# Strassen kernel for a gated FNet and FFN mix: second-level couples moved from product 3 to product 4 of the output stage, evictions at high priority, a longer warm-up of short matmuls

## The chip, the cores and the metric

The kernel runs on one core of a Trainium2 chip. The metric is the device time of one execution in microseconds (us), lower is better; a run's time includes about 2 us outside the span that the profile covers. All times here are of the chip.

## What is computed

The reference mixes two transforms of the same x (2048 x 1024) row by row with a gate; F is 3584:

```python
x = A_x                                                  # S = 2048, D = 1024
g = _sigmoid((x * gate_w).sum(-1, keepdims=True))
# A: real part of a DFT over the hidden dimension, then over the sequence
a = jnp.einsum("bsd,ed->bse", x, dft_hid_re)
b = jnp.einsum("bsd,ed->bse", x, dft_hid_im)
y = jnp.einsum("ts,bse->bte", dft_seq_re, a) - jnp.einsum("ts,bse->bte", dft_seq_im, b)
# B: dense, squared relu, dense
h = jnp.einsum("bsd,df->bsf", x, w1) + b1
h = jnp.where(h > 0, h, 0) ** 2
out = jnp.einsum("bsf,fd->bsd", h, w2) + b2
return g * y + (1 - g) * out
```

All of it is in fp32.

## The kernel before

**Precision.** Each operand is split into a high part (`hi`, rounded to the matmul format by ScalarE, L220) and the rest (`lo`, by VectorE, L230). A product of two operands is three matmuls, hi·hi, hi·lo and lo·hi (L299 to L304), each of a 128x128 stationary and a 128x512 moving tile into a PSUM tile `ps`. Narrow operands of 256 columns hold both parts in one tile, `both`: its first half is written by ScalarE, its second by VectorE.

**Strassen.** Every stage multiplies with the seven products of Strassen and Winograd, in the order 1, 2, 5, 6, 3, 7, 4 (L19). Operands of a product are blocks or sums of blocks (S1 to S4, T1 to T4), made by VectorE (L172) from loaded blocks (L152, SyncE's queue). Results of a product are added to output blocks that stay in SBUF. Some products use a second level of Strassen on some couples of the inner dimension K (`twice`): `TWICE_O = {2: 3, 3: 3}` (L20) says that in the output stage products 2 and 3 do so on 3 couples each. The stage has 7 steps of K, hence 3 couples and one step left over. A couple at the second level saves 12 of 96 matmuls. The rest of a product goes step by step (`direct`), a step being 24 matmuls.

**Stages.** In order: the DFT over the hidden dimension (1224 matmuls), the DFT over the sequence ("spectral stage", `c_stage`, 2580, with the second level on 4 couples in product 2, 3 in product 3 and 2 in product 4), the first dense layer in two parts (1224 and 936), the second dense layer ("output stage", `o_stage`, 2280). Together 8244 matmuls of L304. Ahead of them stand 8 matmuls on a tile of ones (`WARM`, L905), which compute nothing that is used.

**Second level of a product, in two phases** (`twice`). First phase: k couples, each as four steps of 12 matmuls, into four groups (second-level products 1, 6, 7, 5). As each group ends, its PSUM block goes to the output: product 1 by ScalarE's copy to a temporary u (L490) and VectorE's add (L444), product 6 and 7 each by two adds (L501, then L503), product 5 by L444, L526 and L529. Second phase: three groups (products 2, 3, 4) and the steps that are left, on PSUM tiles that are first filled ("prefilled") from those output blocks by ScalarE (L292), so that TensorE adds on top of them. For this place the text speaks of the switch of a product.

**Evictions.** When a group ends, its callback (`done`) is run from `Group.run`: ScalarE copies PSUM to SBUF (`put`, L438 and, in the wide stages, L606), VectorE adds PSUM to a block (`add`, L444 and L613), or the block is finished: `final` (L841 twice, L844, then a store from GpSimd's queue, L943), and in the last group of the output stage `last` row by row (L828, L830 and a store each, L831). `Group.prepare` takes PSUM tiles and prefills them.

**Order.** The main loop (L916 to L973) goes through the steps; at each it issues loads, sums and splits of later steps as planned costs and free slots allow (`SLOTS` 55 tiles), then the step's matmuls. The tile framework's scheduler then orders each engine's instructions by priority, which follows the order of the program unless a block asks for another. Engines run their instructions in order; a waiting instruction holds all behind it on its engine.

**Far sums.** With `FAR_TALL = ("T2",)`, sum T2 of a right operand is stored to DRAM by GpSimd's queue when it is made and loaded again when a later sum needs it (L127, `far`); `early("T4")` (L466 to L467) instead makes T4 during product 6 and stores that, for the first 2·k steps of K if product 4 has k couples at the second level.

Of the kernel before, what the change touches and what calls it, by code (L numbers as in the profile page):

```python
# [11 lines left out]
AF = mybir.ActivationFunctionType  # L12
ALU = mybir.AluOpType

P = 128
# [1 line left out]
NF = F // P  # L17
SLOTS, KEEP, RAWS = 55, 5, 4
WIDE, TALL_C, TALL_O = ((1, 2, 5, 6, 3, 7, 4),) * 3  # L19
TWICE_X, TWICE_C, TWICE_O = (1, 2, 5, 3, 4), {2: 4, 3: 3, 4: 2}, {2: 3, 3: 3}  # L20
LATER = 3
WARM = 8
FAR_TALL, FAR_WIDE = ("T2",), ()
TWICE_H = (1, 2, 5, 3, 4), (2, 5, 3, 4)
SUMS, RESTS, LOADS, SPREAD = 3, 2, 12, 9
# [16 lines left out]
def gated_mix_kernel(ctx: ExitStack, tc: tile.TileContext, x4, xn, w4, ct, w1a, w1b, w2, b1, b2, gw, out):  # L42
# [11 lines left out]
    nc = tc.nc  # L54

    const = ctx.enter_context(tc.tile_pool(name="const", bufs=1))
# [49 lines left out]
    class View:  # L106
# [6 lines left out]
        done = property(lambda self: self.base.done)  # L113
# [150 lines left out]
    class Group:  # L264


        def __init__(self, rows, k, *done, onto=None, sign=1, by_row=False):

            self.sign, self.per = float(sign), 1 if by_row else 2
# [6 lines left out]
        def prepare(self):  # L279

            if not all(b.begun for b in self.onto or ()):
                return
            for k in range(len(self.ps), -(-self.rows // self.per)):
                if not banks or self.per == 2 and len(banks) < -(-self.rows // 2) - k:
                    break
                self.pools.append(banks.popleft())
                t = self.pools[-1].tile([P, 2, 512], F32, name="ps", tag="ps")
                self.ps.append(t)
                if self.onto:
                    n = min(self.per, self.rows - self.per * k)  # L290
                    at = self.per * k % 2
                    nc.scalar.activation(t[:, :n, :], self.onto[self.per * k // 2].slot[:, at:at + n, :], AF.Copy,  # L292
                                         scale=self.sign)

        def run(self, st, mv, by_part=False):
            self.prepare()
            self.at += 1
            ends = self.at % self.k == 0
            mms = [(r, kk, n) for r in range(self.rows) for kk in range(2) for n in range(3)]  # L299
            if by_part:  # L300
                mms.sort(key=lambda e: (e[1], e[0] // 2, e[2], e[0]) if e[1] == 0 else (e[1], e[2], e[0]))
            for r, kk, n in mms:
                a, b = ((st.hi, mv.hi), (st.hi, mv.lo), (st.lo, mv.hi))[n]
                nc.tensor.matmul(self.ps[r // self.per][:, r % self.per, :], a[:, kk, r * P:(r + 1) * P],  # L304
                                 b[:, kk, :], start=self.at == 1 and kk + n == 0 and not self.onto,
                                 stop=ends and kk == 1 and n == 2,
                                 skip_group_check=bool(self.at > self.k or self.onto))
                if ends and self.per == 1 and kk == 1 and n == 2:
                    self.done[0][0](r // 2, self.ps[r], r % 2)
                elif ends and (r % 2 or r == self.rows - 1) and kk == 1 and n == 2:  # L310
                    self.done[self.at // self.k - 1][0](r // 2, self.ps[r // 2])
            if self.at == self.k * len(self.done):
                banks.extend(self.pools)

# [49 lines left out]
    def seven(order, second, new_u, c11, c12, c21, c22, put, add, direct, twice, slots, sign=1):  # L364

        one, u = new_u(), new_u()
        before = {p: order[:order.index(p)] for p in order}

        def product(p, old, new, ends, slots, drop=False, sign=1):
            if p in second:  # L370
                twice(p, old, new, ends, drop, sign)
                return

            def take_up(k, ps):
                put(new, k, ps, ends, sign)
                if drop:
                    old[k].drop()

            direct(p, old, slots, take_up, [new], sign)

        def six(k, ps):
            put(u, k, ps)
            add(c12, k, ps, 3 in before[6], c22, sign)
            if 2 in before[6]:
                one[k].drop()

        def seven(k, ps):
            add(c22, k, ps, True, None, sign)
            if 4 in before[7]:
                add(c21, k, ps, True)  # L390
                u[k].drop()
            else:
                put(u, k, ps)

        ends = {}
        for p in order:
            if p == 1:
                product(1, None, one, False, slots)
            elif p == 2:
                product(2, one, c11, True, slots, 6 in before[2])  # L400
            elif p == 3:
                product(3, c12, c12, True, 0, sign=sign)
            elif p == 4 and 7 in before[4]:
# [12 lines left out]
        return ends  # L416

    def tall(left, right, ksteps, order, second, target, final, last=None):
# [10 lines left out]
        c11, c12, c21, c22 = ({k: target(i, n, k) for k in keys} for i in range(2) for n in range(2))  # L429
# [18 lines left out]
                near.done = True  # L448
                later.append((now[0] + LATER, lambda: final(near, None)))

        def direct(p, onto, slots, take_up, into, sign):
            l, r = FACTORS[p]
            end = last and p == order[-1]

            def take_row(rp, ps, row):
                last(into[0][1, rp], ps, row)
                if row:
                    onto[1, rp].drop()

            groups = [Group(4, ksteps, (take_row if end and c else lambda rp, ps, c=c: take_up((c, rp), ps), slots,  # L460
                                        [d[c, rp] for d in into for rp in range(2)]),
                            onto=onto and [onto[c, rp] for rp in range(2)], by_row=end and c) for c in range(2)]
# [115 lines left out]
    def wide(left, right, rows, order, second, target, final, sign=1, onto_old=False):  # L578
# [14 lines left out]
        c11, c12, c21, c22 = ({k: target(i, n, k) for k in keys} for i in range(2) for n in range(2))  # L593
# [24 lines left out]
                near.done = True  # L618
                later.append((now[0] + LATER, lambda: final(near, None, 1)))

        def direct(p, onto, slots, take_up, into, sign):
            l, r = FACTORS[p]
            mvs = [[right[q, c].operand(r) for q in range(2)] for c in range(2)]
            for m in range(2):
                sts = [left[m, q].operand(l, rows * P) for q in range(2)]
                for c in (m, 1 - m):
                    group = Group(rows, 2, (lambda rp, ps, m=m, c=c: take_up((m, c, rp), ps), slots,
                                             [d[m, c, rp] for d in into for rp in range(2)]),
                                  onto=onto and [onto[m, c, rp] for rp in range(2)], sign=sign)
                    for q in range(2):  # L630
                        step(sts[q], mvs[c][q], group)

# [228 lines left out]
    at, rows = c_stage()  # L861
# [13 lines left out]
    n = len(steps)  # L875
# [26 lines left out]
    nc.vector.memset(ones, 1.0)  # L902
    idle = banks[-1].tile([P, 2, 512], F32, name="ps", tag="ps")
    for _ in range(WARM):
        nc.tensor.matmul(idle[:, 0, :], ones[:, :P], ones, start=True, stop=True)  # L905
# [105 lines left out]
```

## Time and profile before

| | before |
|---|---|
| median of 3 runs | 1890.89 us (1890.39 to 1891.28) |
| profiled execution, its time | 1891.5 us |
| its span | 1889.6 us |
| TensorE busy | 1878.5 us, 99% |
| VectorE busy | 1610.7 us, 85% |
| ScalarE busy | 999.9 us, 53% |
| mean DMA rate over the span | 234 GB/s |

In the profile PE is TensorE's matmuls, PEld its weight loads, DVE VectorE, ACT ScalarE, POOL GpSimd, SP SyncE; a name with q is an engine's queue of DMA issues. A row of the timeline has the start and length in us, the engine, line and operation, the tiles written and read, the shape and the count of instructions merged; in brackets the idle time before it and what released it. A matmul's length reaches over the start of the next one, so rates are read from starts. A row of a wait lists the total, the times and the longest. Stages by first matmul: the first stage at 6.1 us, the spectral stage at 288, the dense layer's parts at 876 and 1153, the output stage at 1367 with its products 2 at 1443, 5 at 1511, 6 at 1588, 3 at 1664, 7 at 1732 and 4 at 1808 to 1884.

### The profile page before, as it was taken

To read this page: it belongs to the slowest core of one execution; us is meant where nothing else is said; L and a number is where in the kernel's file an instruction comes from. 1 tells how busy PE (TensorE), PEld (TensorE's weight loads), DVE (VectorE), ACT (ScalarE), POOL (GpSimd) and SP (SyncE) were. 2 spreads that over 40 slices of the span, in tenths; PEclk is the share of its full clock that TensorE was granted. 3 is DMA by queue.
4 is the path that set the end of the run, shared out by engine and by line. 5 is a ranking of instruction groups with operands and counts; after the bars stand their busy time and mean duration, and the time that the engine had idled before them with its cause. 6 is when DMAs were issued, how large, how long until landed. Compare 5 with 4: busy or idle time off the path is not lost.

```text
span 1889.6 us, 21909 instructions
## 1 busy us (share of the span) xinstructions
PE 1878.5 (99%) x8252; PEld 1548.7 (82%) x8252; DVE 1610.7 (85%) x1543; ACT 999.9 (53%) x1123; POOL 86.8 (5%) x161
## 2 busy tenths in 40 slices
PE   9999999999999999999999999999999999999998
PEld 6888888888888878888888888888888888888887
DVE  8998899499778998798896997989976996699883
ACT  7474564363243554455484797667954434364440
POOL 0000110000000000000000000000100000000000
PEclk9999999999999999999999999999999999999999
DMA  5732889339687489483452865627863886549971
GB/s 223 259 110 88 345 294 407 132 114 378 257 307 263 154 306 357 172 312 112 164 189 71 330 215 199 225 89 294 292 260 100 316 334 241 188 157 361 410 307 45
DMA packets 128425, 442.93 MB, mean 234 GB/s; under 512 B 14128, under 2 KB 23616, under 8 KB 128320
## 3 DMA queue, kind: packets, MB, share of 16 engines
q1 hardware_dynamic: 106272, 363.13, 53.0%
q0 software_dynamic: 21472, 77.61, 10.4%
q8 instruction: 65, 1.06, 0.2%
q10 hardware_dynamic: 576, 0.79, 0.1%
q14 instruction: 40, 0.33, 0.1%
HBM read 362.83 MB, written 78.65 MB: 234 GB/s over the span
## 4 chain that ended last, share of the span: by engine, by line
PE 54%; issue 40%; POOL 2%; ACT 1%; DVE 1%; DMA 1%; SPq 0%; POOLq 0%; DVEq 0%; ACTq 0%
PE ps L304 54%; POOL h L127 1%; ACT hi L220 1%; DVE lo L230 1%; DMA raw<-in_x 0%; DMA raw<-in_ct 0%; POOL copy L127 0%; POOL gy L127 0%; DMA h<-h 0%; DVE h L613 0%; ACT u L606 0%; DVE o L828 0%; DVE o L830 0%; DVE raw L172 0%; SPq L152 0%
## 5 line engine op out<-in xcount | busy, mean ns | idle before, releaser
L304 PE MATMUL ps<-hi 128*128 128x512 f32 x2328 | 906.1, 390 | 2.6 <-ACT u L606 1.1
L304 PE MATMUL ps<-lo,hi 128*128 128x512 f32 x2328 | 905.4, 389 | 0.0
L304 PE MATMUL ps<-hi,lo 128*128 128x512 f32 x2328 | 904.6, 389 | 0.7 <-DVE lo L230 0.6
L220 ACT ACTIVATE hi<-raw 128x1024 fp32r<-128x1024 f32 (+2 forms) x413 | 419.9, 1037 | 410.2 <-DVE raw L172 268.0
L230 DVE TENSOR_TENSOR lo<-raw,hi 128x1024 fp32r<-128x1024 f32 (+2 forms) x413 | 484.6, 1200 | 57.1 <-ACT hi L220 33.0
L304 PEld LDWEIGHTS ps<-hi 128*128 128x128 f32 x2328 | 437.3, 188 | 95.9 <-ACT hi L220 2.7
L304 PEld LDWEIGHTS ps<-hi,lo 128*128 128x128 f32 x2328 | 437.4, 188 | 93.1 <-DVE lo L230 2.2
L304 PEld LDWEIGHTS ps<-lo,hi 128*128 128x128 f32 x2328 | 437.5, 188 | 90.7 <-DVE lo L230 0.2
L172 DVE TENSOR_TENSOR raw<-raw 128x1024 f32<-128x1024 f32 (+1 forms) x276 | 326.6, 1207 | 55.8 <-DMA raw<-in_ct 19.7
L220 ACT ACTIVATE hi<-sum 128x1024 fp32r<-128x1024 f32 (+1 forms) x172 | 175.5, 1035 | 194.6 <-DVE sum L172 151.4
L304 PE MATMUL ps<-hi,both 128*128 128x512 f32 x840 | 260.5, 390 | 1.2 <-ACT ps L292 1.2
L230 DVE TENSOR_TENSOR lo<-sum,hi 128x1024 fp32r<-128x1024 f32 (+1 forms) x172 | 203.4, 1199 | 32.4 <-ACT hi L220 24.9
L304 PEld LDWEIGHTS ps<-hi,both 128*128 128x128 f32 x840 | 157.7, 188 | 35.9 <-ACT ps L292 2.6
L304 PE MATMUL ps<-lo,both 128*128 128x512 f32 x420 | 163.7, 390 | 0.1
L172 DVE TENSOR_TENSOR sum<-raw 128x1024 f32<-128x1024 f32 (+1 forms) x116 | 122.2, 1067 | 36.9 <-PE ps L304 31.6
L172 DVE TENSOR_TENSOR sum<-raw,sum 128x1024 f32<-128x1024 f32 (+2 forms) x87 | 96.8, 1120 | 14.4 <-PE ps L304 11.6
L606 ACT ACTIVATE u<-ps 128x1024 f32<-128x1024 f32 x76 | 72.0, 952 | 69.2 <-PE ps L304 60.9
L613 DVE TENSOR_TENSOR h<-h,ps 128x1024 f32<-128x1024 f32 x92 | 98.1, 1086 | 11.8 <-ACT u L606 10.0
L304 PEld LDWEIGHTS ps<-lo,both 128*128 128x128 f32 x420 | 78.8, 188 | 16.7 <-DVE lo L230 0.5
L292 ACT ACTIVATE ps<-u 128x1024 f32<-128x1024 f32 (+1 forms) x74 | 70.2, 954 | 27.2 <-DVE o L841 10.5
L710 ACT ACTIVATE h<-h,b1c 128x512 f32<-128x512 f32 x112 | 74.3, 712 | 6.1 <-DVE h L613 5.8
L220 ACT ACTIVATE both<-sum 128x512 fp32r<-128x512 f32 x60 | 37.1, 623 | 45.5 <-DVE sum L172 32.1
(61 smaller groups left out, 648.1 us busy)
## 6 DMA issues: line engine op xcount, KB each, us to landing
raw<-in_ct SPq DMA_DIRECT2D x151, 512.0 KB, 6.5
raw<-h SPq DMA_DIRECT2D x132, 512.0 KB, 7.1
raw<-in_x SPq DMA_DIRECT2D x107, 512.0 KB, 5.3
raw<-in_w SPq DMA_DIRECT2D x98, 512.0 KB, 6.4
raw<-ab SPq DMA_DIRECT2D x72, 512.0 KB, 6.6
h<-h POOLq DMA_DIRECT2D x48, 512.0 KB, 5.4
raw<-in_w1a SPq DMA_DIRECT2D x36, 512.0 KB, 5.4
ab<-ab POOLq DMA_DIRECT2D x32, 512.0 KB, 6.5
```

Source lines behind the costliest of these rows:

```text
L127: nc.gpsimd.dma_start(self.at[:, k:k + tiles, :], src[:, :tiles, :])
L172: nc.vector.tensor_tensor(self.slot[:, k, c], src[0][:, k, c], src[1][:, k, c], op=self.op)
L220: nc.scalar.activation(self.hi[:, k, c], self.block.slot[:, k, c], AF.Copy)
L230: nc.vector.tensor_tensor(self.lo[:, k, c], self.block.slot[:, k, c], self.hi[:, k, c].bitcast(F32), op=SUB)
L292: nc.scalar.activation(t[:, :n, :], self.onto[self.per * k // 2].slot[:, at:at + n, :], AF.Copy, scale=self.sign)
L304: nc.tensor.matmul(self.ps[r // self.per][:, r % self.per, :], a[:, kk, r * P:(r + 1) * P], b[:, kk, :], start=self.at == 1 and kk + n == ...
L606: nc.scalar.activation(view(near.slot, k), view(ps, k), AF.Copy, scale=float(sign))
L613: nc.vector.tensor_tensor(view(near.slot, k), view((src or dst)[k].slot, k), view(ps, k), op=ADD if sign > 0 else SUB)
L710: nc.scalar.activation(dst.slot[:, k, :], (dst.slot if ps is None else ps)[:, k, :], AF.Relu, bias=b1c[:, tile0 + k:tile0 + k + 1])
```

## The change

Five things are changed together.

1. `TWICE_O` becomes `{2: 3, 3: 2, 4: 2}`: in the output stage product 3 has the second level on 2 couples of K, not 3, and product 4, the last one, on 2, not on none. The last group of the kernel, finished row by row, is then the second level's block (1, 1) with 2 rows; before it was a half of product 4 with 4 rows. T4 is made early, in product 6, for 4 steps of K.
2. `WARM` becomes 44, on a tile of ones of 128x128: each warming matmul has 128 columns, not 512.
3. Evictions (the callbacks `done`) and ScalarE's prefills are issued under `tc.high_priority(100)`.
4. A block that a group is prefilled from is dropped when it has been copied to PSUM (`spend`), not when the group's result is taken up; the slots that product 7 asks for change accordingly.
5. The first loads go out in another order and on other queues: w part 0, x part 1, w part 1 and x part 2 on SyncE's, x part 0 on ScalarE's; before, both w parts and x part 2 on SyncE's, x parts 0 and 1 on ScalarE's.

```diff
-TWICE_X, TWICE_C, TWICE_O = (1, 2, 5, 3, 4), {2: 4, 3: 3, 4: 2}, {2: 3, 3: 3}
+TWICE_X, TWICE_C, TWICE_O = (1, 2, 5, 3, 4), {2: 4, 3: 3, 4: 2}, {2: 3, 3: 2, 4: 2}
 LATER = 3
-WARM = 8
+WARM = 44
+AHEAD, AHEAD_P = 100, 100
...
-        def __init__(self, rows, k, *done, onto=None, sign=1, by_row=False):
+        def __init__(self, rows, k, *done, onto=None, spend=False, sign=1, by_row=False):
...
-                    nc.scalar.activation(t[:, :n, :], self.onto[self.per * k // 2].slot[:, at:at + n, :], AF.Copy,
-                                         scale=self.sign)
+                    b = self.onto[self.per * k // 2]
+                    with tc.high_priority(AHEAD_P):
+                        nc.scalar.activation(t[:, :n, :], b.slot[:, at:at + n, :], AF.Copy, scale=self.sign)
+                    if self.spend and (self.per == 2 or at):
+                        b.drop()
...
-                if ends and self.per == 1 and kk == 1 and n == 2:
-                    self.done[0][0](r // 2, self.ps[r], r % 2)
-                elif ends and (r % 2 or r == self.rows - 1) and kk == 1 and n == 2:
-                    self.done[self.at // self.k - 1][0](r // 2, self.ps[r // 2])
+                if not (ends and kk == 1 and n == 2):
+                    continue
+                with tc.high_priority(AHEAD):
+                    if self.per == 1:
+                        self.done[0][0](r // 2, self.ps[r], r % 2)
+                    elif r % 2 or r == self.rows - 1:
+                        self.done[self.at // self.k - 1][0](r // 2, self.ps[r // 2])
...
-                direct(6, one, 2 * slots, six, [u, c12], 1)
+                direct(6, one, 2 * slots, six, [u, c12], 1, 2 in before[6])
             else:
-                direct(7, u, 0, seven, [u, c22, c21], 1)
+                direct(7, u, slots * (4 not in before[7]), seven, [u, c22, c21], 1, True)
...
-    run(first[0].load_parts(cycle((nc.sync,))), first[2].load_parts(iter((nc.scalar, nc.scalar, nc.sync))))
-    ones = const.tile([P, 512], mybir.dt.bfloat16, name="ones")
+    w_parts, x_parts = first[0].load_parts(cycle((nc.sync,))), first[2].load_parts(iter((nc.scalar, nc.sync, nc.sync)))
+    for parts in (w_parts, x_parts, x_parts, w_parts, x_parts):
+        next(parts)
+    run(w_parts, x_parts)
+    ones = const.tile([P, P], mybir.dt.bfloat16, name="ones")
     nc.vector.memset(ones, 1.0)
     idle = banks[-1].tile([P, 2, 512], F32, name="ps", tag="ps")
     for _ in range(WARM):
-        nc.tensor.matmul(idle[:, 0, :], ones[:, :P], ones, start=True, stop=True)
+        nc.tensor.matmul(idle[:, 0, :P], ones, ones, start=True, stop=True)
```

More of the change, by code (lines that the diff above doesn't have):

```diff
@@ L264, in gated_mix_kernel @@
     class Group:
-        def __init__(self, rows, k, *done, onto=None, sign=1, by_row=False):
-            self.sign, self.per = float(sign), 1 if by_row else 2
+        def __init__(self, rows, k, *done, onto=None, spend=False, sign=1, by_row=False):
+            self.sign, self.per, self.spend = float(sign), 1 if by_row else 2, spend
             self.rows, self.k, self.done, self.at, self.onto = rows, k, done, 0, onto
@@ L372, in product @@
                 return
[L374 to L379, printed above, removed]
+            direct(p, old, slots, lambda k, ps: put(new, k, ps, ends, sign), [new], sign, drop)
         def six(k, ps):
@@ L383, in six @@
             add(c12, k, ps, 3 in before[6], c22, sign)
-            if 2 in before[6]:
-                one[k].drop()
         def seven(k, ps):
@@ L390, in seven @@
                 add(c21, k, ps, True)
-                u[k].drop()
             else:
@@ L449, in add, with direct @@
                 later.append((now[0] + LATER, lambda: final(near, None)))
-        def direct(p, onto, slots, take_up, into, sign):
+        def direct(p, onto, slots, take_up, into, sign, spend=False):
             l, r = FACTORS[p]
             end = last and p == order[-1]
[L455 to L460, printed above, removed]
+            groups = [Group(4, ksteps, ((lambda rp, ps, row: last(into[0][1, rp], ps, row)) if end and c else
+                                        lambda rp, ps, c=c: take_up((c, rp), ps), slots,
                                         [d[c, rp] for d in into for rp in range(2)]),
-                            onto=onto and [onto[c, rp] for rp in range(2)], by_row=end and c) for c in range(2)]
+                            onto=onto and [onto[c, rp] for rp in range(2)], spend=spend, by_row=end and c) for c in range(2)]
             sts = {q: left[q].operand(l) for q in range(ksteps)}
@@ L619, in add, with direct @@
                 later.append((now[0] + LATER, lambda: final(near, None, 1)))
-        def direct(p, onto, slots, take_up, into, sign):
+        def direct(p, onto, slots, take_up, into, sign, spend=False):
             l, r = FACTORS[p]
@@ L628, in direct @@
                                              [d[m, c, rp] for d in into for rp in range(2)]),
-                                  onto=onto and [onto[m, c, rp] for rp in range(2)], sign=sign)
+                                  onto=onto and [onto[m, c, rp] for rp in range(2)], spend=spend, sign=sign)
                     for q in range(2):
```

## The prediction

> Line numbers are those of the kernel before; "matmul" without more is one of L304, and lengths are in us.
>
> **What bounds the kernel now.** I read the page's busy times first, then TensorE's waits, then the timeline at each place where TensorE stood.
>
> ```profile
> span 1889.6 us, 21909 instructions
> PE 1878.5 (99%) x8252; PEld 1548.7 (82%) x8252; DVE 1610.7 (85%) x1543; ACT 999.9 (53%) x1123; POOL 86.8 (5%) x161
> L220 ACT ACTIVATE hi<-sum 128x1024 fp32r<-128x1024 f32 (+1 forms) x172 | 175.5, 1035 | 194.6 <-DVE sum L172 151.4
> PE ps L304 <- ACT ps L292: 1.5, 3, 0.6
> PE ps L304 <- ACT u L606: 1.1, 1, 1.1
> PE ps L304 <- DVE lo L230: 0.6, 2, 0.5
> ```
>
> (The third row, a group of the page with its mean of 1035 ns, is used further down.) TensorE is busy 99% of the span: the number of matmuls sets the time. It runs 8252 of them, 8 for warming and 8244 of L304. The waits (total, times, longest) are short; VectorE, at 85%, is the engine that could become the next bound. A busy row is longer than the distance between two matmuls, so the price of a matmul is read from starts. Product 4 of the output stage is the last one, 336 matmuls long, and nothing stops it:
>
> ```profile
> 1808.16 0.39 PE L304 MATMUL ps<-hi 128*128 128x512 f32 x1
> 1884.10 0.39 PE L304 MATMUL ps<-hi,lo 128*128 128x512 f32 x1
> ```
>
> From its first start to its last, 335 distances take 75.94, so one is 0.2267. All 8244 at that price are 1868.9. The first starts at 6.10 (below) and 5.5 follow the last start up to 1889.6; together 1880.5. Only some 9 are left for a cold clock and for stalls: what can be won without taking matmuls away is at most that.
>
> **The change, part by part.** The profiled run took 1891.5, 1.9 more than its span, and lies 0.6 above the median of 1890.89. I sum changes of the span and put them on the median.
>
> *Count.* In the output stage product 3 has one couple fewer (12 matmuls more), product 4 has two couples (24 fewer): 8232 matmuls, 12 x 0.2267 = **-2.7**. The loads of SyncE and the copies of GpSimd keep their number; the tail is still two rows of L828, L830 and a store, so its 5.5 stay. VectorE gets 8 sums and 8 splits more; product 4 is 70.7 long instead of 76.2.
>
> *Start.* 44 short bf16 matmuls replace 8 long ones, and the second load on ScalarE's queue goes to SyncE's.
>
> ```profile
> 1.46 3.59 PE L905 MATMUL ps<-ones 128*128 128x512 bf16 x8 [1.46 <-DVE ones L902]
> 1.86 0.15 PEld L905 LDWEIGHTS <-ones 128*128 128x128 bf16 x1 [0.28 <-issue]
> 6.10 1.22 PE L304 MATMUL ps<-hi 128*128 128x512 f32 x2 [1.05 <-ACT hi L220]
> ...
> 10.88 1.09 PE L304 MATMUL ps<-hi 128*128 128x512 f32 x4
> ...
> 13.67 0.50 PE L304 MATMUL ps<-hi 128*128 128x512 f32 x1
> 15.41 1.92 ACT L606 ACTIVATE u<-ps 128x1024 f32<-128x1024 f32 x2
> 22.08 0.50 PE L304 MATMUL ps<-hi 128*128 128x512 f32 x1 [1.13 <-ACT u L606]
> ```
>
> A warming matmul of 512 columns takes 0.43 (its weight load 0.15 and the 0.28 between two loads); a quarter of the columns is 0.107 if the weight load stays hidden, so 44 are 4.7 and end near 6.1. If nothing is hidden each is 0.107 + 0.15 = 0.257, 11.3 in all, ending near 12.7. Here weight loads run under other matmuls (82% of the span), so I take the first, which closes the gap of 1.05. From 6.10 to 10.88 twelve matmuls take 4.78 where 2.72 would do: 2.06 is what the slow clock costs. Not all of it comes back. In the changed order ScalarE evicts the first two blocks (1.92) before it splits the operand of the second step (1.04), so that step starts 0.4 + 1.92 + 1.04 = 3.4 after the first step's end, where it followed at once. A first step ending near 11.5 lets the second begin near 14.9, later than 13.67; but the wait of 22.08, for the same evictions, is gone. Walked so, VectorE's splits set the pace up to the fourth step and **-0.4** is left; bounds -2.1 - 1.1 = -3.2 (clock and wait all gained) and +5 (weight loads in the open).
>
> In the Trainium skill, "TensorE: Matmul & The Clock Gate", section "Part 1: The HAM clock gate", 128-column matmuls in a row stand 107 ns apart cold and about 56 warm, and the clock rises by a free-running window of about 3.4 us, not by a count. The trace agrees in that the clock rose after 10 us, behind the gap; by the page the start would gain the 2.06 if nothing followed, and my sum would be 1.7 lower.
>
> *Evictions ahead.* The order of VectorE's and ScalarE's instructions moves where blocks end. Three stalls lie there:
>
> ```profile
> 660.79 0.61 PE L304 MATMUL ps<-hi,both 128*128 128x512 f32 x2
> 661.94 0.50 PE L304 MATMUL ps<-hi,both 128*128 128x512 f32 x1 [0.54 <-ACT ps L292]
> 663.07 0.50 PE L304 MATMUL ps<-hi,both 128*128 128x512 f32 x1 [0.63 <-ACT ps L292]
> ...
> 1299.95 0.39 PE L304 MATMUL ps<-hi,lo 128*128 128x512 f32 x1
> ...
> 1302.54 0.39 PE L304 MATMUL ps<-hi 128*128 128x512 f32 x1
> ...
> 1363.36 0.39 PE L304 MATMUL ps<-lo,hi 128*128 128x512 f32 x1
> 1363.90 0.50 PE L304 MATMUL ps<-hi,lo 128*128 128x512 f32 x1 [0.15 <-DVE lo L230]
> ```
>
> At 661 product 3 of the spectral stage changes from its second-level blocks to those that are prefilled (L292): from 660.79 three distances (0.68) take 2.28, a loss of 1.6. In the changed order two more instructions of VectorE (about 1.7) come before the evictions and one (0.6) moves out ahead, which makes the first prefill up to 1.1 later; but nine matmuls (2.0) instead of one stand between the first and the second prefilled block, which hides the second. I take -0.3, bounds -0.9 and +1.7. At 1300 six distances (1.36) take 2.59, a loss of 1.2 to a prefill behind VectorE's adds; they come earlier, but TensorE no longer puts six matmuls of the next product between: -0.3, bounds -1.2 and +0.5. At 1363 0.54 instead of 0.23: -0.3, since the split there comes earlier. Together **-0.9**.
>
> *The switch inside the new product 4.* This decides. When a second-level product ends its first phase, VectorE has a fixed chain: L444, L503, L526, then L529, with splits between; the next blocks are prefilled from its results. The twin is product 4 of the spectral stage, also with two couples, and TensorE has no wait there:
>
> ```profile
> 815.99 1.22 DVE L444 TENSOR_TENSOR y<-y,ps 128x1024 f32<-128x1024 f32 x1 [0.21 <-PE ps L304]
> 817.13 1.22 DVE L503 TENSOR_TENSOR y<-u 128x1024 f32<-128x1024 f32 x1
> 818.26 1.22 DVE L526 TENSOR_TENSOR y<-u,ps 128x1024 f32<-128x1024 f32 x1
> 819.40 0.69 DVE L172 TENSOR_TENSOR sum<-raw,sum 128x512 f32<-128x512 f32 x1
> 820.00 1.22 DVE L529 TENSOR_TENSOR y<-y,u 128x1024 f32<-128x1024 f32 x1
> 821.13 1.22 DVE L230 TENSOR_TENSOR lo<-raw,hi 128x1024 fp32r<-128x1024 f32 x1
> 822.27 0.69 DVE L230 TENSOR_TENSOR both<-sum,both 128x512 fp32r<-128x512 f32 x1
> 817.25 2.16 ACT L292 ACTIVATE ps<-y 128x1024 f32<-128x1024 f32 x2 [4.67 <-DVE y L444]
> ```
>
> The chain goes at 1.13 to 1.14 an instruction, 0.60 for a half. In the twin's order the first split behind it is used 62 matmuls after the one that ended the phase, 14.1 later: ample. In the order that the scheduler makes of the new product 4 it is L444, L503, L526, a split (lo), L529, a split (both), and after the last matmul of the phase TensorE starts on the block prefilled from L503 with the 14th, uses that lo with the 15th and that both with the 16th. With time from the start of that last matmul: L444 can start at 0.39; five instructions at 1.135 and one of 0.69 end at 6.76. TensorE gets there after 16 distances, 3.63, if nothing holds it. Loss **+3.1**. The prefill from L503 alone would cost less: L503 ends at 0.39 + 1.13 + 1.22 = 2.7, ScalarE needs about 1.08, done 3.8 against 14 distances, 3.2. Everything used after that is ready in time by the same count (next: split at 8.5, used at 9.3), so nothing gives the 3.1 back: the matmuls behind it follow at their pace to the end. Bounds: 0 (as the twin), and 4.3 if VectorE comes to L444 1.2 late, by one instruction.
>
> *VectorE in the rest of it.* Windows of before (length, PE, PEld, DVE, ACT, POOL, clock, DMA share, GB/s):
>
> ```profile
> 1727.00:1804.00 77.00, 77.00 (x341) 63.78 (x340) 66.19 (x60) 32.31 (x31) 2.89 (x4) 1.00 1.00 388
> 1804.00:1884.00 80.00, 80.00 (x355) 66.26 (x354) 48.41 (x50) 20.06 (x21) 4.28 (x6) 1.00 0.42 163
> ```
>
> From the first eviction of product 7, some 8 before product 4 starts, the changed order holds about 75 of VectorE's work, against 53 (its instructions by the distances above); up to the end there are 8 + 70.7 + 1.4 = 80. It fits with 5 spare, so the switch finds VectorE hardly late. I cost it at nothing; without that cover its excess is the slower rival. In product 7 the same work has 13 more to go into, since product 3's switch comes 48 matmuls earlier; its small stall, about 0.2, goes:
>
> ```profile
> 1699.33 0.39 PE L304 MATMUL ps<-lo,both 128*128 128x512 f32 x1
> 1699.68 0.50 PE L304 MATMUL ps<-hi,both 128*128 128x512 f32 x1
> 1700.02 0.39 PE L304 MATMUL ps<-lo,both 128*128 128x512 f32 x1
> ```
>
> Two distances take 0.69 there instead of 0.45: **-0.2**. The earlier T4 sums go to product 6, where VectorE has room; the copies they need meet DMA engines at a share of 1.00 in product 7, where they must have landed: nothing, bounds 0 and +2.
>
> Sum: -2.7 - 0.4 - 0.9 + 3.1 - 0.2 = **-1.1**; 1890.9 - 1.1 = **1889.8**.
>
> **The rivals.** (a) *Switch hidden*: the stall in product 4 is as small as its twin's, and the start gives what the clock takes. -2.7 - 2.1 - 0.9 - 0.2 = -5.9: 1885.0. For it: the twin and the three-couple switch at 1699 lose next to nothing. Against: the distance of 16 matmuls is fixed in the order, and VectorE has 1.135 a step everywhere. (b) *Last product bound by VectorE*, the other side: two couples put 75 of work where 53 was; if DMA, at 1.00 in product 7, lets the operands land late, VectorE's 5 spare are lost first, and each us more delays TensorE. It decides once VectorE is 5 late at the switch; at 10 late the loss there is 3.1 + 5 = 8.1, and the sum +3.9: 1894.8. For it: VectorE's windows here; against: SyncE's loads are no more than before, and product 7 gains 13. (c) *Warm-up in the open*: each short matmul waits for its weights, the start loses up to 5, sum +4.3: 1895.2. For it: the 0.15 of the weight load is longer than 0.107. Against: loads run under matmuls everywhere else. (d) *Stalls only move*: evictions ahead cost elsewhere what they save; the 0.9 and the 0.4 drop out: +0.2, 1891.1.
>
> **How the numbers follow.** Forecast 0.45, (a) 0.17, (d) 0.16, (b) 0.12, (c) 0.10. The range reaches to (a) and (b): 1885.0 to 1894.8. A difference under 0.2% (3.8, so 1887.1 to 1894.7) can't be told from none. Within are the forecast, without 0.04 that its bounds send to the faster and 0.02 to the slower side, and (d): 0.39 + 0.16 = 0.55; faster 0.17 + 0.04 = 0.21; slower 0.22 + 0.02 = 0.24.
>
> **What would show it.** In the profile after: 8232 matmuls; a first real matmul near 6.1 and a clock up before 8; a wait of product 4's matmuls for a split of VectorE (lo, both) of about 3 in all, some 50 before the end of the span; the row at 1363 gone, and less than 1.6 lost at 661. The prediction is wrong if TensorE has no wait in the last 70 us, if VectorE has no idle time in product 4 up to its last splits, or if the first real matmul starts after 8.

## The result, and the profile after

| | before | after |
|---|---|---|
| median, 16 runs each | 1891.03 us | 1894.87 us |
| lowest to highest | 1890.39 to 1892.55 | 1893.27 to 1897.41 |
| ratio, 95% interval | | 1.0019 (1.0012 to 1.0025) |
| span of the profiled execution | 1889.6 | 1892.9 |

The changed kernel is 3.8 us slower, 0.07 outside the predicted range, on the side that was given a chance of 0.24. Its span is 3.3 longer. The page after and its list of TensorE's waits (total, times, longest):

```profile
span 1892.9 us, 21971 instructions
PE 1877.2 (99%) x8276; PEld 1549.9 (82%) x8276; DVE 1631.2 (86%) x1566; ACT 1008.2 (53%) x1131; POOL 87.6 (5%) x162
```

```profile
PE ps L308 <- ACT hi L221: 3.9, 2, 3.3
PE ps L308 <- DVE lo L231: 2.2, 3, 1.2
PE ps L308 <- DVE both L231: 1.2, 1, 1.2
PE ps L308 <- ACT ps L295: 1.1, 1, 1.1
PE ps L903 <- DVE ones L900: 1.1, 1, 1.1
PE ps L308 <- DVE h L608: 0.8, 2, 0.5
```

8276 less 44 warming matmuls are the 8232 that were counted. L308, L231, L221, L295 and L608 are L304, L230, L220, L292 and L613 of before. Ahead of the change most waits were for prefills (L292) and evictions (L606); now they are for splits, of ScalarE (hi) and VectorE (lo, both), that is, for operands of the next matmuls. The row of L903 is the warm-up.

Where the 3.3 come from, place by place. "Lost" is the sum, over the starts of consecutive matmuls, of the distance less 0.2267, where that is 0.1 or more.

| place | lost before | lost after | difference | predicted |
|---|---|---|---|---|
| matmuls left out | | | -2.7 | -2.7 |
| start, first four steps | 4.6 | 5.3 | +0.7 | -0.4 |
| 661 to 672, switch of product 3 of the spectral stage | 2.2 | 0 | -2.2 | -0.3 |
| 1300 to 1318, dense layer | 1.2 | 3.0 | +1.8 | -0.3 |
| 1363, end of the dense layer | 0.4 | 0.4 | 0 | -0.3 |
| 1699, product 3 of the output stage | 0.2 | 0 | -0.2 | -0.2 |
| product 4 of the output stage | 0 | 5.4 | +5.4 | +3.1 |
| tail, last start to end | 5.5 | 5.8 | +0.3 | 0 |

Together +3.1; the 0.2 that are left lie in distances too small for the list. The largest row is the switch of product 4. TensorE there, after:

```profile
1835.34 0.61 PE L308 MATMUL ps<-hi,both 128*128 128x512 f32 x2
1837.02 0.50 PE L308 MATMUL ps<-hi,both 128*128 128x512 f32 x1 [1.07 <-ACT ps L295]
1838.22 0.49 PE L308 MATMUL ps<-lo,both 128*128 128x512 f32 x1 [0.70 <-DVE lo L231]
1839.96 0.74 PE L308 MATMUL ps<-hi,both 128*128 128x512 f32 x2 [1.24 <-DVE both L231]
...
1841.42 0.63 PE L308 MATMUL ps<-lo,both 128*128 128x512 f32 x1
1841.84 1.05 PE L308 MATMUL ps<-hi,both 128*128 128x512 f32 x2
1842.70 0.63 PE L308 MATMUL ps<-lo,both 128*128 128x512 f32 x1
```

and VectorE beside it:

```profile
1832.42 1.22 DVE L496 TENSOR_TENSOR u<-u,ps 128x1024 f32<-128x1024 f32 x1
1833.55 1.22 DVE L443 TENSOR_TENSOR o<-o,ps 128x1024 f32<-128x1024 f32 x1
1834.68 1.23 DVE L498 TENSOR_TENSOR o<-u 128x1024 f32<-128x1024 f32 x1
1835.81 1.22 DVE L521 TENSOR_TENSOR o<-u,ps 128x1024 f32<-128x1024 f32 x1
1836.94 1.23 DVE L231 TENSOR_TENSOR lo<-sum,hi 128x1024 fp32r<-128x1024 f32 x1
1838.08 1.23 DVE L524 TENSOR_TENSOR o<-o,u 128x1024 f32<-128x1024 f32 x1
1839.21 0.69 DVE L231 TENSOR_TENSOR both<-raw,both 128x512 fp32r<-128x512 f32 x1
```

The chain is the predicted one, instruction by instruction. It runs from 1833.55 to 1839.90, 6.35 where 6.37 were counted, and TensorE waits for the three things in it that were named: the prefill, lo, both. Two things come on top. VectorE has no idle time in front of L443 and comes to it 0.5 late: the last matmul of the phase stands 13 ahead of the one at 1835.56, so it started at 1832.6 and L443 could have at 1833.0. And behind the wait matmuls stand 0.43 apart, not 0.23 (1841.42 to 1841.84 is one distance, 1841.84 to 1842.70 are two): the slow clock, 8 of them, 1.6. Wait 3.8, clock 1.6, sum 5.4.

Windows of product 4, in the columns of the prediction's:

```profile
1811.20:1835.60 24.40, 24.40 (x110) 20.16 (x108) 24.32 (x27) 14.61 (x18) 2.15 (x3) 1.00 0.64 220
1835.60:1860.00 24.40, 21.39 (x85) 16.74 (x84) 24.40 (x26) 9.92 (x12) 0.00 (x0) 0.93 0.64 233
1860.00:1887.00 27.00, 27.00 (x121) 22.36 (x120) 15.05 (x17) 3.25 (x4) 2.14 (x3) 1.00 0.16 59
```

VectorE (the third busy time) has nothing left in the first 49 us, 24.32 and 24.40 of 24.40, and 12 idle in the last 27. The prediction named this as a sign of being wrong: before its last split VectorE stands idle only once for more than 0.1, for 1.13 at 1866.24. It never waits for a load in the first 49 us, so late loads are not what makes it late; DMA is busy for 0.64 there. The clock of the middle window is 0.93.

### The profile page after: what moved, and what is told of

Read it like the earlier page. It is cut to its first block, busy times and chain, and to the rows that moved or that the text cites. A ratio compares the mean times of both kernels' runs of the same rounds, so it can differ in the third digit from the quotient of the medians.

```text
span 1892.9 us, 21971 instructions
## 1 busy us (share of the span) xinstructions
PE 1877.2 (99%) x8276; PEld 1549.9 (82%) x8276; DVE 1631.2 (86%) x1566; ACT 1008.2 (53%) x1131; POOL 87.6 (5%) x162
## 5 line engine op out<-in xcount | busy, mean ns | idle before, releaser
L308 PE MATMUL ps<-hi 128*128 128x512 f32 x2296 | 893.0, 390 | 4.7 <-ACT hi L221 3.9
L308 PE MATMUL ps<-lo,hi 128*128 128x512 f32 x2296 | 893.0, 389 | 1.5 <-DVE lo L231 1.5
L308 PE MATMUL ps<-hi,lo 128*128 128x512 f32 x2296 | 891.8, 389 | 0.0
L221 ACT ACTIVATE hi<-raw 128x1024 fp32r<-128x1024 f32 (+2 forms) x410 | 418.3, 1038 | 412.2 <-DVE raw L173 244.8
L231 DVE TENSOR_TENSOR lo<-raw,hi 128x1024 fp32r<-128x1024 f32 (+2 forms) x410 | 480.8, 1200 | 56.2 <-ACT hi L221 26.7
L308 PEld LDWEIGHTS ps<-hi 128*128 128x128 f32 x2296 | 431.1, 188 | 95.9 <-ACT hi L221 5.0
L308 PEld LDWEIGHTS ps<-lo,hi 128*128 128x128 f32 x2296 | 431.2, 188 | 92.2 <-DVE lo L231 3.0
L308 PEld LDWEIGHTS ps<-hi,lo 128*128 128x128 f32 x2296 | 431.1, 188 | 90.5 <-DVE lo L231 0.5
L221 ACT ACTIVATE hi<-sum 128x1024 fp32r<-128x1024 f32 (+1 forms) x176 | 180.2, 1037 | 203.0 <-DVE sum L173 169.1
L308 PE MATMUL ps<-hi,both 128*128 128x512 f32 x896 | 278.8, 391 | 2.3 <-DVE both L231 1.2
L231 DVE TENSOR_TENSOR lo<-sum,hi 128x1024 fp32r<-128x1024 f32 (+1 forms) x176 | 208.2, 1199 | 37.2 <-PE ps L308 19.1
L308 PEld LDWEIGHTS ps<-hi,both 128*128 128x128 f32 x896 | 168.8, 188 | 39.1 <-ACT ps L295 2.0
L308 PE MATMUL ps<-lo,both 128*128 128x512 f32 x448 | 175.2, 391 | 0.7 <-DVE lo L231 0.7
L608 DVE TENSOR_TENSOR h<-h,ps 128x1024 f32<-128x1024 f32 x92 | 98.5, 1085 | 7.9 <-ACT u L601 7.1
L308 PEld LDWEIGHTS ps<-lo,both 128*128 128x128 f32 x448 | 84.5, 189 | 18.4 <-DVE lo L231 1.0
L295 ACT ACTIVATE ps<-u 128x1024 f32<-128x1024 f32 x68 | 65.6, 973 | 19.1 <-DVE o L836 6.1
L221 ACT ACTIVATE both<-sum 128x512 fp32r<-128x512 f32 x64 | 39.4, 624 | 51.6 <-DVE sum L173 33.9
```

The source lines that it names most:

```text
L221: nc.scalar.activation(self.hi[:, k, c], self.block.slot[:, k, c], AF.Copy)
L231: nc.vector.tensor_tensor(self.lo[:, k, c], self.block.slot[:, k, c], self.hi[:, k, c].bitcast(F32), op=SUB)
L295: nc.scalar.activation(t[:, :n, :], b.slot[:, at:at + n, :], AF.Copy, scale=self.sign)
L608: nc.vector.tensor_tensor(view(near.slot, k), view((src or dst)[k].slot, k), view(ps, k), op=ADD if sign > 0 else SUB)
```

## The experiments

Each experiment was timed beside the kernel before, whose medians were 1890.98 (the first four), 1891.05 (spend_only to late_rest_back) and 1891.01 (the last three). "Lost" is as above. A span is that of one execution, the profiled one, which can lie off the median of its version (by 2.4 below in late, by 1.9 above in couples_only): what a version is worth is read from medians, and where it loses from the trace.

### no_ahead: the changed kernel without the priorities

```diff
-AHEAD, AHEAD_P = 100, 100
+AHEAD, AHEAD_P = 0, 0
```

> The changed kernel with both priorities of evictions and prefills set to 0, all else kept. Theory (the priority puts L443, L498, L521 and L524 ahead of the two splits at the switch of product 4): in this order the splits stand ahead of the adds, so TensorE loses under 1 us at the switch instead of 3.8, and there is no stretch of slow clock behind it (1.6). The gain at 661 stays (it comes from the earlier drop of blocks, item 4), the losses at 1308 and 1316 (2.2) go and some 1.2 at 1300 come back; the start stays. Span 1892.9 - 5.0 - 1.8 + 0.6 = about 1886.5, time about 1888.5. Rival (two couples load VectorE too much in the last product, whatever the order): 3 to 5 us are lost in product 4 still, span 1890 to 1892.

Measured: 1892.13, ratio 1.0008 (0.9999 to 1.0017), span 1889.3. Lost at 661: nothing; at 1300: 1.2, with nothing at 1308 and 1316; at the start 5.6. So far as expected. In product 4, 4.2 instead of under 1:

```profile
1835.48 0.50 PE L308 MATMUL ps<-hi,both 128*128 128x512 f32 x1 [1.82 <-ACT ps L295]
...
1841.84 0.74 PE L308 MATMUL ps<-hi,both 128*128 128x512 f32 x2 [0.40 <-DVE both L231]
...
1844.84 0.50 PE L308 MATMUL ps<-hi,both 128*128 128x512 f32 x1 [0.17 <-ACT both L221]
...
1851.57 0.50 PE L308 MATMUL ps<-hi 128*128 128x512 f32 x1 [0.49 <-ACT hi L221]
```

With the splits ahead of the adds the prefill is late instead (2.1 with its after-effects), and three small waits for splits follow (2.1). VectorE is busy without a gap there too:

```profile
1808.30:1833.30 25.00, 25.00 (x112) 20.65 (x111) 24.91 (x29) 14.30 (x18) 2.16 (x3) 1.00 0.66 230
1833.30:1857.00 23.70, 20.83 (x87) 15.72 (x86) 23.70 (x24) 9.98 (x11) 0.00 (x0) 1.00 0.64 232
```

The order decides which wait is longest, not that there is one: the rival, VectorE's load, held for product 4, although the span is 0.7 under the 1890 to 1892 that it gave.

### couples_back: the changed kernel with the couples of before

```diff
-{2: 3, 3: 2, 4: 2}
+{2: 3, 3: 3}
```

> The changed kernel with the second level of the output stage as before (3 couples in product 3, none in product 4), all else kept. Theory: the 5.4 us lost at the switch of product 4 go, 12 matmuls (2.7) come back, product 3's small stall (0.2) too: span 1892.9 - 5.4 + 2.9 = 1890.4, so the couples cost 2.5 us together with the priority. Rival (the loss comes from the rest of the change, the start and the dense layer, and the couples are a gain): span above 1893.

Measured: 1891.63, ratio 1.0002 (0.9993 to 1.0011), span 1890.5, as expected to 0.1, which is in part luck: this execution lies 0.9 above the median, and its start loses 0.9 more than that of the changed kernel. Nothing is lost in product 4. The new couples cost 3.2 of the median (2.4 of the span), although they save 12 matmuls.

### couples_only: the kernel before with the new couples

```diff
-{2: 3, 3: 3}
+{2: 3, 3: 2, 4: 2}
```

> The kernel before with the new couples of the output stage alone. Theory: without the priority the order at the switch has the splits ahead of the last adds, TensorE loses under 1 us there, so 12 matmuls and product 3's stall are won: span 1889.6 - 2.9 + 0.5 = 1887.2. Rival (VectorE's load in the last product): 3 to 5 us lost at the switch, span 1890 to 1892.

Measured: 1894.90, ratio 1.0020 (1.0011 to 1.0029), span 1895.0. The theory failed by 8 us. Its wait list begins so:

```profile
PE ps L304 <- ACT ps L292: 6.2, 7, 1.8
PE ps L304 <- ACT hi L220: 3.2, 3, 1.4
```

Product 4 loses 4.9 (2.0 for a prefill, then nine matmuls at the slow clock, 1.7, and 1.2 of smaller waits); 3.1 are lost at 661 instead of 2.2, 2.2 in product 6 and 0.7 in product 3 of the output stage, all of them prefills, behind VectorE or behind a split whose sum waited for its load. The new couples thus cost 3.9 of the median without any priority. (The stage at 661 is the same program in both; its loss differs by 0.9 between executions.)

### start_back: the changed kernel with warm-up and first loads of before

```diff
-WARM = 44                     # on ones[128, 128]
+WARM = 8                      # on ones[128, 512]
-    w_parts, x_parts = ...     # w0 SP, x0 ACT, x1 SP, w1 SP, x2 SP
+    run(first[0].load_parts(cycle((nc.sync,))), first[2].load_parts(iter((nc.scalar, nc.scalar, nc.sync))))
```

> The changed kernel with the warm-up (8 matmuls of 512 columns) and the first loads as before. Theory: ScalarE's order at the second step (both evictions ahead of the split) stays, since the priority alone makes it, so the wait of about 3.4 us stays and the first step is slow again: the start loses 2 more, span 1892.9 + 2 = 1895. Rival (the warm-up or the loads make the wait): the second step follows at once, start as before, span about 1892.2.

Measured: 1896.2, ratio 1.0025 (1.0016 to 1.0034), span 1894.0. The start loses 7.5, 2.2 more than in the changed kernel, as expected in size. Not for the expected reason: the clock was up from the third matmul on, with the old warm-up, and the waits of 3.3 and 1.1 at the second step were followed by 11 slow matmuls, 2.2. In this version, with the priority, the new warm-up and loads are thus 1.3 of the median better than the old ones.

### spend_only and ahead_only: items 4 and 3 on the kernel before

```diff
+                    if self.spend and (self.per == 2 or at):
+                        b.drop()               # spend_only, with the drops of take_up, six and seven removed
...
+                    with tc.high_priority(100):   # ahead_only, around prefills and around done(...)
```

> The kernel before with item 4 alone (a block is dropped when it has been copied to PSUM). Theory: the 2.2 us lost at 661 to 672 go, since TensorE has nine matmuls between the two prefilled blocks there, and nothing else moves: span 1889.6 - 2.2 = 1887.4. Rival (the loss at 661 went with the priority): span 1889.6.

> The kernel before with the two priorities alone. Theory: ScalarE evicts ahead of the second step's split (start +1.5 us), the dense layer loses 1.8 more at 1300 to 1317, the 2.2 at 661 stay: span 1889.6 + 3.3 = about 1893. Rival (the priority is harmless where VectorE isn't late): span within 1 of 1889.6.

spend_only: 1888.77, ratio 0.9988 (0.9979 to 0.9997), span 1886.7. The loss at 661 (2.2) is gone, which is the gain of the median, 2.3; in the profiled execution the losses at 1363 (0.4) and 1699 (0.2) are missing too, hence 2.9 of span. TensorE at 661:

```profile
660.81 0.84 PE L308 MATMUL ps<-hi,both 128*128 128x512 f32 x3
661.49 0.39 PE L308 MATMUL ps<-lo,both 128*128 128x512 f32 x1
661.72 0.62 PE L308 MATMUL ps<-hi,both 128*128 128x512 f32 x2
662.17 0.39 PE L308 MATMUL ps<-lo,both 128*128 128x512 f32 x1
```

No row has idle time; before, two waits of 0.54 and 0.63 stood here. By the program, a block that is free earlier lets the loop plan the operands of the next steps earlier, and TensorE has nine matmuls of another block while ScalarE prefills the second.

ahead_only: 1896.58, ratio 1.0029 (1.0018 to 1.004), span 1895.3, worse than expected by 2.3: start 6.9 lost (1.5 was expected on top of 4.6, 2.3 were found), dense layer 4.0 (at 1150 and 1303 to 1323), 661 2.6. Of the three items that were run alone (the couples, the priority, the earlier drop) the priority is the worst; it costs 5.5 of the median.

### late and late_rest_back: finals put off past the switch

```diff
-                later.append((now[0] + LATER, lambda: final(near, None)))
+                later.append((now[0] + (14 if last and dst is c22 and src is None else LATER), lambda: final(near, None)))
```

late is the changed kernel with this edit; late_rest_back also has AHEAD 0 and the old warm-up and first loads.

> The changed kernel with the finals of product 7's four blocks (some 10 us of VectorE's work: L836, L839) put off by 14 steps instead of 3, past the switch of product 4; the priorities stay at 100. Theory (VectorE is late at the switch since finals, sums and splits all fall into product 4's first 50 us; only a late VectorE lets the priority put the adds ahead of the splits): in this order the splits stand ahead of the adds, under 0.5 us are lost in product 4 instead of 5.4, span 1892.9 - 5 = 1888. Rival (the priority itself makes the stall): 3.1 us and the slow clock behind it stay, span 1892 to 1893.

> The new couples, the earlier drop and the finals put off as in the run beside it, but no priorities, and the warm-up and first loads of before. Theory (sum of the single effects): count -2.7, product 3's stall -0.2, the loss at 661 -2.2, product 4 at most +0.5: span 1889.6 - 4.6 = 1885.0, time 1886.3, faster than both kernels. Rival (what is won at one place is lost at the next wait): span 1887 to 1889.

late: 1889.74 (1887.38 to 1893.24), ratio 0.9993 (0.9984 to 1.0001), span 1885.4 (of the fastest of its runs); its median is 5.1 below that of the changed kernel. Product 4 loses 1.0 instead of 5.4, none of it at the switch, with the priorities still at 100. Of the four blocks' finals three moved past the switch, 7.4 us of VectorE's work, not the 10 that were expected; the first block's still run from 1801.60 to 1808.76. VectorE after the switch, in late:

```profile
1839.94 1.41 DVE L836 SCALAR_TENSOR_TENSOR o<-o,b2c,g 128x512 f32<-128x512 f32 x2
...
1842.40 1.22 DVE L839 TENSOR_TENSOR o<-o,raw 128x1024 f32<-128x1024 f32 x1
...
1844.67 2.07 DVE L836 SCALAR_TENSOR_TENSOR o<-o,b2c,g 128x512 f32<-128x512 f32 x3
```

With these out of the way VectorE has made the splits that the first matmuls behind the switch need before the adds are due, and there is nothing for the priority to put them behind: VectorE's rows at the switch, 1823.93 to 1837.60, are the same in late and late_rest_back, to 0.01. The 1.0 is one wait at 1852, for a high part whose sum stands behind finals that come there now. The span is 2.6 under the 1888 expected; 1.5 of that lies in the dense layer and 0.4 at 1363, places that the edit does not touch.

late_rest_back: 1887.03, ratio 0.9980 (0.9971 to 0.9989), span 1885.4, expected 1885.0, time 0.7 over the 1886.3 expected; this version beats both kernels.

### late20, more_couples, late_start_new: on top of late_rest_back

late20 puts the finals off by 20 steps; more_couples has `{2: 3, 3: 3, 4: 2}`; late_start_new has the new warm-up and first loads.

> The version of late_rest_back with the finals of product 7 put off by 20 steps instead of 14. Theory (VectorE's finals cost TensorE time only where they stand ahead of splits): the 1.0 lost at 1852 to a split behind finals goes, span 1885.4 - 0.9 = 1884.5. Rival (the finals now run into product 4's last splits and its own finals): as much is lost there, span 1885.4 or more.

> The version of late_rest_back with 3 couples left in product 3 as before, so the second level is on 3 couples in product 3 and on 2 in product 4: 8220 matmuls. Theory: 12 matmuls less, -2.7, product 3's small stall of 0.2 comes back: span 1885.4 - 2.5 = 1882.9. Rival (VectorE has no room for both products): a stall of 2 or more in products 3, 7 or 4 takes it back, span 1885 or more.

> The version of late_rest_back with the warm-up of 44 short matmuls and the changed first loads. Theory (they change ScalarE's order so that both evictions stand ahead of the second step's split, and the clock is up early in most executions anyway): the start costs some 5.5 instead of 4.5, span 1885.4 + 1 = 1886.4. Rival (a warm clock from the first step on is worth its 2): span 1883.5 to 1885.

late20: 1886.02, ratio 0.9971 (0.9961 to 0.9981), span 1884.3: nothing is lost in product 4, though its tail is 6.3 long instead of 5.7, and all its runs lie between 1885.6 and 1886.6. It is the best version found, 5.0 faster than before. Its windows of product 4:

```profile
1804.50:1829.00 24.50, 24.50 (x110) 20.29 (x109) 24.36 (x28) 16.02 (x21) 0.71 (x1) 1.00 0.48 171
1829.00:1853.00 24.00, 24.00 (x108) 19.71 (x107) 24.00 (x24) 11.80 (x12) 0.00 (x0) 1.00 0.65 242
1853.00:1880.00 27.00, 25.47 (x113) 20.77 (x111) 20.46 (x24) 1.66 (x2) 4.30 (x6) 1.00 0.33 124
```

VectorE is as full as before in the first two, but 20.46 instead of 15.05 lie in the last, and TensorE is busy in every one. So it is not a full VectorE that costs time, but work that could wait standing ahead of what TensorE needs next. (The third window ends 1.5 behind TensorE's last matmul, hence its 25.47.)

more_couples: 1887.69, ratio 0.9981 (0.9972 to 0.9990), span 1884.5 for 1882.9 expected. Product 4 loses 3.1 in two waits, at 1848 and 1850, each for a high part of a sum that VectorE makes behind finals; product 3 loses 0.5. The rival held in kind, though the span it named was 1885 or more: 12 matmuls less bring nothing here.

late_start_new: 1887.91, ratio 0.9985 (0.9976 to 0.9994), span 1886.1. The start loses 5.7 for 4.4: the new warm-up and loads cost 1.3 there, 0.7 of the span and 0.9 of the median, where no priority is set. They were never changed apart from each other, so which of the two costs is open. Beside no_ahead (1892.13) this version differs by the finals alone: put off, they are worth 4.2 without the priority. Beside late it differs by the priority alone, which still costs 1.8.

## Why the prediction was wrong, point by point

The forecast for the span was -1.1, and +3.3 was measured. Of the 4.4 between them 2.3 lie in product 4, 2.1 in the dense layer, 1.1 at the start, 0.3 at 1363, 0.3 in the tail and 0.2 in small distances, while 661 gave 1.9 more than was forecast. Three steps failed: VectorE's load around the last switch and the slow clock behind a wait, both put at nothing, and the gain of the evictions in the dense layer, which was a loss. That the time ends so close to the range is luck: the gain at 661, which has another cause than the one given, makes up for 1.9.

*Count*, right: -2.7, and the tail is 0.3 longer.

*VectorE in the rest of it*: this step failed. The prediction put 75 of VectorE's work against 80 of time over the whole of product 4 and costed the load at nothing. The sum fits (VectorE's work from there to the end is 73.7 in the trace), but the work doesn't lie evenly: finals of product 7, sums and splits of both second-level phases and the adds of the switch all fall into the first 49 us, where VectorE has 0.1 idle, and 12 of the spare time lie in the last 27, too late for that stretch. Moving 7.4 us of finals behind the switch took 4.4 of the 5.4 away (late), moving them further the 1.0 that late_rest_back still loses (late20). This was rival (b) in kind, but its condition, loads that land late, was not what happened: VectorE waited for none there.

*The switch inside the new product 4*: mechanism and place right, size 5.4 for 3.1. The chain was 6.35 for 6.37; what was missing is 0.5 of VectorE's lateness and its after-effects (wait 3.8), and 1.6 of slow clock behind the wait, a term that the sum did not have. But the reason given, a fixed order, was only half of it: with the splits in front (no_ahead) 4.2 are lost all the same, and with the load moved nothing is lost at the switch, with the priority (late) or without it (late_rest_back).

*Start*: -0.4 predicted, +0.7 measured. The prediction saw that ScalarE evicts ahead of the split of the second step, and the rows bear it out:

```profile
12.41 1.92 ACT L601 ACTIVATE u<-ps 128x1024 f32<-128x1024 f32 x2
14.22 1.06 ACT L221 ACTIVATE hi<-sum 128x1024 fp32r<-128x1024 f32 x1
```

```profile
1.07 4.32 PE L903 MATMUL ps<-ones 128*128 128x128 bf16 x44 [1.07 <-DVE ones L900]
...
10.97 1.07 PE L308 MATMUL ps<-hi,lo 128*128 128x512 f32 x4
15.32 0.80 PE L308 MATMUL ps<-hi 128*128 128x512 f32 x1 [3.29 <-ACT hi L221]
15.92 0.63 PE L308 MATMUL ps<-lo,hi 128*128 128x512 f32 x1
16.35 0.63 PE L308 MATMUL ps<-hi 128*128 128x512 f32 x1
```

The 44 matmuls end at 5.39, the first step ends early as walked, and the second begins at 15.32 (14.9 predicted). What the walk left out is that the wait of 3.3 gives the slow clock back: 0.63 long and 0.43 apart, about 1.3 in all. The runs show more: the start loses 4.4 to 4.6 with the old order whether the first matmuls are slow (before, late20) or the clock is up at the third (spend_only, late_rest_back). Its pace is set by the first operands, so a fast clock in the first step won nothing there; rival (c), weight loads in the open, is out, as 44 took 4.32.

*Evictions ahead*: -0.9 predicted, -0.4 measured as the sum of two errors. The gain at 661 was 2.2 instead of 0.3 and came from item 4, not from the priority (spend_only has it, ahead_only does not). The wait for a split at 1363 went, but one of 0.27 for an eviction came at 1364.39. In the dense layer 0.3 of gain were 1.8 of loss, and ahead_only loses 2.8 more there than the kernel before. After, at 1316:

```profile
1314.32 0.96 DVE L173 TENSOR_TENSOR raw<-raw 128x768 f32<-128x768 f32 x1 [1.87 <-DMA raw<-in_w1b]
1315.19 1.81 DVE L608 TENSOR_TENSOR h<-h,ps 128x1024 f32<-128x1024 f32 x2
1316.92 2.09 DVE L231 TENSOR_TENSOR lo<-raw,hi 128x1024 fp32r<-128x1024 f32 x2
1318.19 0.50 PE L308 MATMUL ps<-lo,hi 128*128 128x512 f32 x1 [1.21 <-DVE lo L231]
```

VectorE stands 1.87 on a sum whose load has not landed, then the eviction (1.7) goes ahead of the split, and TensorE waits 1.21 for that split. This is rival (d), stalls that move, and the loss is larger than the one removed. VectorE's order there is the same in late. Where the execution loses about 3 (after, couples_back, ahead_only), VectorE's wait for this load is 1.87, 1.72 and 1.53; where it loses 1.5 to 1.6, it is 0.92 (start_back) or nothing (late), and the wait of TensorE at 1316 is missing. With the priority, then, the wait comes with a late load; in three executions without it (before, no_ahead, late_start_new) VectorE waits for no load there. Why the load lands late in some is open.

*The rivals*: slower by over 0.2% had 0.24, and 3.84 lies on the very bound of 3.8. (a), the switch hidden, needed the finals put off (late, late_rest_back, late20). (d) held for the dense layer alone.

## What to carry to other kernels

Weigh an engine's load over each stretch between the points where its results are due, not over a stage: spare time after a full stretch is worth nothing to it. Priority for evictions takes time from the splits that the next matmuls wait for; before raising it, move work that nobody waits for (here the finals of finished blocks) out of the full stretch. At the switch the priority then no longer mattered, though the version was still slower with it. And try the items of a bundle singly: here a buffer given back early paid at once (-2.3 of the median), the couples only together with finals put off, which the bundle had not (late20, 2.7 more), and the priority cost in each of three pairs (5.5 alone, 2.7 in the bundle, 1.8 with the finals put off). The new warm-up and loads cost 0.9 without the priority and won 1.3 with it: an item's worth can hang on another's.

## What the runs showed of the hardware that was not expected

A wait of TensorE can cost more than its length, because the clock can fall in it. The changed kernel, in windows with the columns of the others:

```profile
14.89:18.30 3.41, 2.98 (x7) 2.13 (x8) 3.41 (x4) 3.41 (x5) 0.00 (x0) 0.50 1.02 405
18.30:1841.02 1822.72, 1817.40 (x8007) 1501.32 (x8006) 1582.85 (x1515) 986.72 (x1107) 85.21 (x155) 1.00 0.64 236
1841.02:1844.43 3.41, 3.41 (x10) 2.64 (x9) 3.41 (x5) 0.15 (x1) 0.00 (x0) 0.50 0.90 280
```

The granted clock is 0.50 for 3.41 at the second step and for 3.41 at the switch, and 1.00 between. The 1822.72 between are 534 times 3.4133, and the 10.24 from the first rise at 4.65 to the first fall are three times that. Slow stretches inside the other executions last 3.41 as well, or twice that (start_back from 15.85, ahead_only from 14.78). So the clock changes at the ends of steps of 3.41 that do not begin with the wait. This fits that one order gave both outcomes at the start. In late_rest_back the waits that end at 13.58 and 15.32 (1.5 and 0.7 lost) lie in one step, 11.96 to 15.37, at whose end the clock fell, for eight matmuls. In spend_only the same two waits are parted by the end of a step at 14.76 (three steps after the clock rose at 4.52), and it did not fall. A step need not be idle throughout: in couples_only TensorE is busy for 1.55 of the 3.40 ahead of the fall at 1840.74. What share is enough is not shown; the wait of 2.0 at the switch in no_ahead was followed by no slow matmul.

The Trainium skill, "TensorE: Matmul & The Clock Gate", section "Part 1: The HAM clock gate", has the clock follow the activity of a free-running window of about 3.4 us; the steps of 3.41 and that one order gives both outcomes agree with it. It also agrees that with the same 8 warming matmuls the clock rose at the third real matmul in some executions and after the tenth in others.

Runs of one version scatter unevenly: 0.6 from lowest to highest for spend_only, 1.0 for late_rest_back and late20, 4.1 after, 5.9 for late. Why is not shown.
